# Attention and mixture of experts on one core: each PSUM ring tile a buffer of its own, four tanhs and then one exponential per unit

## The chip, the cores and the metric

The kernel runs on one core of a Trainium2 chip. The metric is the device time in microseconds (us) of one execution; lower is better. Five engines work beside each other, each in the order of its own program, and wait for each other by semaphores: PE (TensorE, matrix multiplies), ACT (ScalarE, tanh, exponential, copies), DVE (VectorE), POOL (GpSimd) and SP (SyncE, which issues most transfers). Matrix products are written to PSUM, a small memory of eight banks.

## The reference, cut to what matters

Soft-capped attention over 4 batches with 12 heads of 448 rows of width 64, and then a mixture of 8 experts in which each of the 1792 rows goes to one expert.

```python
scores = scale * np.matmul(q, k.transpose(0, 1, 3, 2))
scores = cap * np.tanh(scores / cap)
attn = np.exp(scores - np.max(scores, axis=-1, keepdims=True))
attn = attn / (np.sum(attn, axis=-1, keepdims=True) + 1e-09)
out = np.matmul(attn, v)
...
e_idx = np.argmax(x @ w_gate, axis=1)          # x: the attention's rows
for e in range(8):
    h = np.maximum(x[e_idx == e] @ w1[e], 0.0)
    out[e_idx == e] = gate_w * eom * (h @ w2[e])
```

## The kernel before

The attention comes first and takes about half of the time, the experts follow. The attention runs over 24 *units* (4 batches of 6 pairs of heads); the loop over `u` near the end of the kernel writes out by hand the order in which every engine gets its work, and nothing reorders it later.

In iteration `u`, PE computes the scores of unit `u`, transposed, in four tiles: `qk(u, 0)` to `qk(u, 2)` hold two heads times 448 columns for 128 rows of K each (L349), `qk(u, 3)` the last 64 rows of both heads (L354). ACT takes each tile out of PSUM with a tanh (L356) into `pt`, and an exponential (L336, `exps`) runs in place over `pt`: one over the first four chunks of 448 columns after the second tanh, one over the other three after the fourth. Then PE multiplies the exponentials of the unit *before* with V: `pv(u - 1, c)`, 16 records in the trace (L366), called PV below. Its result is copied out by `u_evac` (DVE in units 0 to 7, ACT from 8 on, L385). POOL adds up the exponentials for the row sums (`presum`, L375 to L380), PE sums them over the partitions on every other unit (`sums`, L399). DVE turns and splits K and Q for later units (L294, L284, L290).

In the iterations of the following batch, `slot(u, ...)` puts the work that ends a batch in between: gate products (`tg`, L446), transposes of the sums (`trec`, L430), of the gates (`pg`, L461) and of finished attention rows (`trow`, L540, which DVE scales by `xr`, L544, and SP writes to memory as `xs`), ranks of the rows within their expert (`trk`, L494), and at the end the gathering of rows for the first expert (`gather`, L806; `tx`, L818).

All these products, scores, PV and the slots' work, take their PSUM tiles from one pool, `ps_s`, with three buffers of two banks each (named A, B and C below). `half()` hands out the two banks of a tile to two different uses, one after the other: the fourth score tile and PV, two row transposes, two gate transposes. Waits are by tile: what is written to the second bank waits until the first bank has been read. Which buffer a tile gets is settled when the program is built.

Of the kernel before, what the change touches and what calls it, by code (L numbers as in the profile page):

```python
# [9 lines left out]
F32 = mybir.dt.float32  # L10
# [4 lines left out]
ACTF = mybir.ActivationFunctionType  # L15
# [7 lines left out]
def tile_kernel(ctx: ExitStack, tc, q, k, v, cap, w_gate, w_ogate, w1, w2, out):  # L23
    nc = tc.nc
    B, H, S, D = q.shape
# [55 lines left out]
    ps_s = att.enter_context(tc.tile_pool(name="ps_s", bufs=3, space=PSUM))  # L81
# [3 lines left out]
    def tbank(shape, name):  # L85
        tpools.append(tpools.pop(0))
        return tpools[-1].tile(shape, F32, tag="t", name=name)
# [9 lines left out]
    NK = 3  # L97
# [37 lines left out]
    def load_k(u):  # L135
        if u >= NU:
            return
        t, src = kks[u % 3], heads(k, u)
        for c in range(2):
            pieces(t[:, 0:NB], src[0], c, nc.sync)  # L140
        for c in range(2, 4):
            pieces(t[:, 0:BK], src[1, 0:SK], c, nc.sync)
        for c in range(2, 4):
            pieces(t[:, BK + 2:BK + 4], src[1, SK:S], c, nc.scalar)

    def load_q(u):
        if u >= NU:
            return
        t = ldp.tile([128, 2, NB, 32], F32, tag="lq", name="lq", bufs=2)
        lo = 1 - u % 2  # L150
        for c in range(4):
            h = c // 2 * NP + u % NP
            pieces(t[:, 1 - lo:].rearrange("p h r a -> p (h r) a"), q[u // NP, h:h + lo + 1].rearrange("h s d -> (h s) d"), c, nc.sync)
        for i in range(1 - lo, 2):
            ldq[u + i - (1 - lo)] = t[:, i]

    def load_v(u):
        if u < NU:
            v_ = heads(v, u)
            load_natural(vvs[u % 3], v_, NK, 128, (nc.sync, nc.sync))  # L160
            load_tails(vvs[u % 3], v_, nc.sync)


    capc = const.tile([128, 1], F32, name="capc")
# [48 lines left out]
    for j in range(2):  # L213
        for z, src in ((0, w_gate), (8, w_ogate)):
            nc.gpsimd.dma_start(
                out=wg[64 * j:64 * j + 64, :, j, z:z + 8],
                in_=src.rearrange("(j p d) e -> j d p e", j=2, d=D)[j],
# [10 lines left out]
                        in_=tabi.rearrange("p n c -> p (n c)")[:, 0:DM // 16])  # L228
# [49 lines left out]
    pl, pt, ut, s1, ups, smt, rec, xr, lg = {}, {}, {}, {}, {}, {}, {}, {}, {}  # L278
# [32 lines left out]
    def turn_next(n):  # L311
        for f, u in turns[:n]:
            f(u)
        del turns[:n]

    pair = []

    def half(new=False):
        if new or not pair:
            t = ps_s.tile([128, 2, 512], F32, tag="s", name="s")  # L320
            pair[:] = [t[:, 0], t[:, 1]]
        return pair.pop(0)

    def prep_first():
        pk = tbank([128, SK + 128], "tk0")
# [5 lines left out]
        pl[0] = planes_of(0, pk, "K", SK + 128) + planes_of(0, pq, "Q", S)  # L331
        scales()

    def exps(u, s):
        x = pt[u][:, 4 * s:min(4 * s + 4, 2 * NK + 1)]
        nc.scalar.activation(out=x, in_=x, func=ACTF.Exp, scale=capc)  # L336

    def qk(u, s):
        KH, KL, QH, QL = pl[u]
        if s == 0:  # L340
            pt[u] = ptp.tile([128, 2 * NK + 1, S], F32, tag="pt", name="pt")
        n = 2 if s < NK else 1
        sl = slice(s * 128, (s + 1) * 128)
        if s < NK:
            ps = ps_s.tile([128, 2, 512], F32, tag="s", name="s")
            for i, (x, y) in enumerate(((KH, QH), (KL, QH), (KH, QL))):
                for j in range(2):
                    h = slice(64 * j, 64 * j + 64)
                    nc.tensor.matmul(ps[:, j, 0:S], lhsT=x[h, sl], rhs=y[h], start=(i == 0), stop=(i == 2))  # L349
            ps = ps[:, :, 0:S]  # L350
        else:
            ps = half(True)[:, 0:S]
            for i, (x, y) in enumerate(((KH, QH), (KL, QH), (KH, QL))):
                nc.tensor.matmul(ps, lhsT=x[:, sl], rhs=y, start=(i == 0), stop=(i == 2))  # L354
            ps = ps.unsqueeze(1)
        nc.scalar.activation(out=pt[u][:, 2 * s:2 * s + n], in_=ps, func=ACTF.Tanh, scale=icap)  # L356
        if s % 2:
            exps(u, s // 2)

    def pv(u, c):  # L360
        P = pt[u]
        V = vvs[u % 3]
        if c == 0:
            ups[u] = half()[:, 0:S]
        for j in range(2):
            nc.tensor.matmul(ups[u][64 * j:64 * j + 64], lhsT=V[:, c, j, :], rhs=P[:, 2 * c + (j if c < NK else 0)],  # L366
                             start=(c == 0), stop=(c == NK))

    def presum(u, s):
        P = pt[u]  # L370
        eng = nc.vector if u >= NU - 2 else nc.gpsimd
        if s == 0:
            a = smp.tile([128, 2, S], F32, tag="pa", name="pa")
            s1[u] = smp.tile([128, 2, S], F32, tag="pb", name="pb", bufs=3)
            eng.tensor_tensor(out=a, in0=P[:, 0:2], in1=P[:, 2:4], op=ALU.add)  # L375
            eng.tensor_tensor(out=s1[u], in0=a, in1=P[:, 4:6], op=ALU.add)  # L376
        else:
            for j in range(2):
                h = slice(64 * j, 64 * j + 64)
                eng.tensor_tensor(out=s1[u][h, j], in0=s1[u][h, j], in1=P[h, 2 * NK], op=ALU.add)  # L380

    def u_evac(u):
        t = utp.tile([128, S], F32, tag="ut", name="ut")
        if UACT <= u < NU - 3 or u == NU - 1:
            nc.scalar.activation(out=t, in_=ups.pop(u), func=ACTF.Copy)  # L385
        else:
            nc.vector.tensor_copy(out=t, in_=ups.pop(u))
        ut[u] = t

    def sums(u):  # L390

        b, p = divmod(u, NP)
        if p % 2 == 0:
            return
        r = p // 2
        if r == 0:
            smt[b] = ps_m.tile([128, S], F32, tag="sm", name="sm")
        for g in range(4):
            nc.tensor.matmul(smt[b][32 * g:32 * g + 32], lhsT=ohc[:, r, :], rhs=s1[u - 1 + g // 2][:, g % 2],  # L399
                             start=(r == 0), stop=(r == NP // 2 - 1))  # L400
# [10 lines left out]
    def end_of_batch(b):  # L411
        def bank(shape, name, m=False):
            if b == B - 1:
                return tbank(shape, name)
            if m:
                return ps_m.tile(shape, F32, tag="sm", name=name)
            x = half()[0:shape[0], 0:math.prod(shape[1:])]
            if len(shape) == 2:
                return x
            k = "abc"[:len(shape) - 1]  # L420
            return x.rearrange(f"p ({' '.join(k)}) -> p {' '.join(k)}", **dict(zip(k, shape[1:])))
# [5 lines left out]
        def sums_tr():  # L427
            ps = rt["trec"] = bank([CP, NCH, 4, 32], "trec", b == B - 2)
            for c in range(NCH):
                nc.tensor.transpose(ps[:, c].rearrange("p j n -> p (j n)"),  # L430
                                    rt["ssb"][:, c * CP:(c + 1) * CP], ident)
# [10 lines left out]
        def gate_mm(r):  # L442
            ps = rt["tg"] = bank([128, S], "tg") if b < B - 1 else moe[0].tile([128, S], F32, tag="hph", name="tg")
            for p in range(*grp[r]):
                o0 = 32 * (p - grp[r][0])
                nc.tensor.matmul(ps[o0:o0 + 32], lhsT=wg[:, p].rearrange("p j e -> p (j e)"),  # L446
                                 rhs=ut[b * NP + p], start=True, stop=True)
# [108 lines left out]
        t = [sums_out, L(sums_tr, recips), L(P(gate_mm, 0), P(gate_out, 0)), L(P(gate_mm, 1), P(gate_out, 1))]  # L556
# [345 lines left out]
    def slot(u, y):  # L902
        for f in slots.pop((u, y), ()):
            f()
# [8 lines left out]
    for u in range(NU):  # L913
        for s in range(NK):
            qk(u, s)
        load_k(u + 3)
        if u % 2:
            load_q(u + 3)
        before, after = TURN.get(u, (1, 1))
        turn_next(before)  # L920
        if u > 0:
            presum(u - 1, 1)
        pair.clear()
        slot(u, "f")
        pair.clear()
        slot(u, "g")
        qk(u, NK)
        slot(u, "h")
        if u > 0:
            for c in range(NK + 1):  # L930
                pv(u - 1, c)
        turn_next(after)
        if u > 1 and u - 2 != EARLY:
            sums(u - 2)
        pair.clear()
        slot(u, "q")
        if u > 0:
            u_evac(u - 1)
        load_v(u + 2)
        presum(u, 0)  # L940
        slot(u, "e")
    pair.clear()
    u = NU - 1
    for s in range(NK):
        pv(u, s)
# [244 lines left out]
    split_to(SP0)  # L1190
    bg.extend(end_of_batch(B - 1))
    pv(u, NK)
    u_evac(u)
    tx(0)
# [97 lines left out]
```

## Time and profile before

| | |
|---|---|
| median of 3 runs | 618.85 us (617.74 to 619.21) |
| the profiled execution's own time | 618.58 us |
| its span, first to last instruction | 616.5 us |
| mean granted TensorE clock (1 is 2.4 GHz, 0.5 is 1.2 GHz) | 0.902 |
| PE busy in the span | 534.1 us, 87% |
| ACT, DVE, POOL busy | 376.6, 376.5, 300.6 us |

PE is the engine with the most work. The busy time of a stretch, what an engine waited for in it, and the clock in it tell more than the share over the span, since attention and experts differ.

### The profile page before, as it was taken

What the parts mean: (1) busy time and instruction counts of PE and PEld (TensorE: products, weight loads), DVE (VectorE), ACT (ScalarE), POOL (GpSimd) and SP (SyncE); (2) the same over time, 40 slices, a digit from 0 to 9 for tenths busy, and PEclk for the clock granted to TensorE, in tenths of its full rate; (3) what the DMA queues carried; (4) which work ended last, traced back from release to release, by engine and by line L of the source; (5) the groups of instructions that cost most, each with busy time, mean ns of one, the idle gap of its engine ahead of it and who ended that gap; (6) DMA issues with size and microseconds to landing.
All of it is one profiled execution on the core that took longest, in us unless ns stands there. A gap on an engine that the chain in (4) does not pass through costs nothing. (4 is left out here: it accounts for less than half of the span.)

```text
span 616.5 us, 10153 instructions
## 1 busy us (share of the span) xinstructions
PE 534.1 (87%) x3053; PEld 352.2 (57%) x3053; DVE 376.5 (61%) x627; ACT 376.6 (61%) x449; POOL 300.6 (49%) x347
## 2 busy tenths in 40 slices
PE   7678767767887877788899999999999999999995
PEld 5233322334343343433368999978887886767593
DVE  4544414247654567554789999868766848646460
ACT  6654554427567466544656678868676858646570
POOL 8756353416766555745457256662163732643001
PEclk9778777769788798877899999999999999999998
DMA  7533314154562554433877079253386796997001
GB/s 136 97 63 58 59 36 70 27 105 69 98 74 45 93 104 75 60 64 79 297 261 242 16 274 407 71 180 136 117 354 234 247 409 216 401 301 306 15 27 42
DMA packets 157773, 91.94 MB, mean 149 GB/s; under 512 B 140418, under 2 KB 140554, under 8 KB 157712
## 3 DMA queue, kind: packets, MB, share of 16 engines
q1 hardware_dynamic: 144032, 57.86, 36.6%
q0 software_dynamic: 8832, 32.74, 14.5%
q10 hardware_dynamic: 4848, 0.63, 0.6%
q8 instruction: 26, 0.43, 0.3%
q14 instruction: 35, 0.29, 0.1%
HBM read 123.68 MB, written 12.04 MB: 220 GB/s over the span
## 5 line engine op out<-in xcount | busy, mean ns | idle before, releaser
L994 DVE TENSOR_TENSOR wr<-raw,wr 128x768 fp32r<-128x768 f32 (+1 forms) x167 | 171.9, 1066 | 64.6 <-ACT wr L993 63.5
L993 ACT ACTIVATE wr<-raw 128x768 fp32r<-128x768 f32 (+1 forms) x167 | 150.4, 936 | 33.9 <-PE py L1015 8.6
L366 PE MATMUL s<-pt,vv 128*64 128x448 f32 x384 | 118.6, 783 | 38.4 <-ACT pt L356 38.4
L356 ACT ACTIVATE pt<-s,icap 128x896 f32<-128x896 f32 x96 | 83.4, 905 | 74.9 <-PE s L349 61.7
L366 PEld LDWEIGHTS s<-pt,vv 128*64 128x64 f32 x384 | 35.8, 195 | 109.6 <-issue 58.4
L336 ACT ACTIVATE pt<-pt,capc 128x1792 f32<-128x1792 f32 (+1 forms) x48 | 76.9, 1603 | 1.6
L1015 PE MATMUL py<-wr,hh 128*128 128x384 f32 x352 | 77.3, 341 | 0.0
L1015 PE MATMUL php<-wr,xh 128*128 128x512 f32 x264 | 74.7, 404 | 0.0
L376 POOL TENSOR_TENSOR pb<-pa,pt 128x896 f32<-128x896 f32 x22 | 46.0, 2092 | 57.1 <-PE sm L399 45.7
L1015 PEld LDWEIGHTS py<-wr,hh 128*128 128x128 f32 x352 | 61.2, 188 | 4.0 <-issue 3.7
L375 POOL TENSOR_TENSOR pa<-pt 128x896 f32<-128x896 f32 x22 | 45.9, 2086 | 34.4 <-ACT pt L336 33.7
L1084 POOL DMA_INDIRECT out_dram<-yo,ti x13 | 18.0, 1384 | 89.0 <-ACT yo L1082 63.6
L1015 PEld LDWEIGHTS php<-wr,xh 128*128 128x128 f32 x264 | 47.5, 188 | 12.1 <-issue 2.1
L380 POOL TENSOR_TENSOR pb<-pb,pt 64x448 f32<-64x448 f32 x44 | 49.9, 1135 | 4.2 <-DMA tab<-ent,posi 0.9
L1015 PE MATMUL py<-wr,hl 128*128 128x384 f32 x176 | 44.8, 335 | 0.0
L294 DVE STREAM_TRANSPOSE tk<-kk 128x512 f32<-128x512 f32 x23 | 16.6, 722 | 42.9 <-DMA kk<-in_k_dram 36.0
L1015 PE MATMUL php<-wr,xl 128*128 128x512 f32 x132 | 41.5, 395 | 0.0
L349 PE MATMUL s<-QH,KH 64*128 64x448 f32 x144 | 30.4, 414 | 9.7 <-ACT pt L356 7.3
L385 ACT ACTIVATE ut<-s 128x448 f32<-128x448 f32 x14 | 7.6, 544 | 46.3 <-PE s L366 46.3
L1131 POOL DMA_DIRECT2D rh<-in_moe_w_dram x42 | 23.2, 555 | 21.8 <-DVE wr L994 13.6
L1015 PEld LDWEIGHTS py<-wr,hl 128*128 128x128 f32 x176 | 31.8, 188 | 0.0
L349 PEld LDWEIGHTS s<-QH,KH 64*128 64x128 f32 x144 | 13.7, 184 | 29.5 <-ACT pt L356 10.6
(262 smaller groups left out, 829.7 us busy)
## 6 DMA issues: line engine op xcount, KB each, us to landing
raw<-in_moe_w_dram SPq DMA_DIRECT2D x78, 512.0 KB
raw<-in_moe_w_dram SPq DMA_DIRECT2D x104, 384.0 KB
rh<-in_moe_w_dram POOLq DMA_DIRECT2D x18, 512.0 KB, 7.6
rh<-in_moe_w_dram POOLq DMA_DIRECT2D x24, 384.0 KB, 9.0
lq<-in_q_dram SPq DMA_DIRECT2D x44, 112.0 KB
vv<-in_v_dram SPq DMA_DIRECT2D x48, 96.0 KB
xs<-xr SPq DMA_DIRECT2D x36, 112.0 KB
kk<-in_k_dram SPq DMA_DIRECT2D x46, 56.0 KB
```

Source lines behind the costliest of these rows:

```text
L336: nc.scalar.activation(out=x, in_=x, func=ACTF.Exp, scale=capc)
L349: nc.tensor.matmul(ps[:, j, 0:S], lhsT=x[h, sl], rhs=y[h], start=(i == 0), stop=(i == 2))
L356: nc.scalar.activation(out=pt[u][:, 2 * s:2 * s + n], in_=ps, func=ACTF.Tanh, scale=icap)
L366: nc.tensor.matmul(ups[u][64 * j:64 * j + 64], lhsT=V[:, c, j, :], rhs=P[:, 2 * c + (j if c < NK else 0)], start=(c == 0), stop=(c == NK))
L375: eng.tensor_tensor(out=a, in0=P[:, 0:2], in1=P[:, 2:4], op=ALU.add)
L376: eng.tensor_tensor(out=s1[u], in0=a, in1=P[:, 4:6], op=ALU.add)
L380: eng.tensor_tensor(out=s1[u][h, j], in0=s1[u][h, j], in1=P[h, 2 * NK], op=ALU.add)
L993: nc.scalar.activation(out=t[:, 0, 0:F], in_=raw, func=ACTF.Copy)
L994: nc.vector.tensor_tensor(out=t[:, 1, 0:F], in0=raw, in1=t[:, 0, 0:F].bitcast(F32), op=ALU.subtract)
L1015: nc.tensor.matmul(ps[g][:, 0:n], lhsT=st[:, c], rhs=w[:, z, g * n:(g + 1) * n], start=(c == 0 and st is hi and z == 0), stop=(c == (KD, K ...
L1084: nc.gpsimd.indirect_dma_start(out=out, out_offset=bass.IndirectOffsetOnAxis(ap=ti, axis=0), in_=y, in_offset=None, bounds_check=NT - 1, o ...
L1131: nc.gpsimd.dma_start(out=d, in_=rows_of(src, e, w, c), **kw)
```

## The change

`half` now takes a whole tile of the ring for each use, and `pair`, which held the second bank back, is gone: PV, each row transpose and each gate transpose have a tile of their own. `exps` is gone: the four tanhs of a unit come one after the other, and one exponential runs over all seven chunks (3136 columns) after the fourth.

```diff
-    pair = []
-
-    def half(new=False):
-        if new or not pair:
-            t = ps_s.tile([128, 2, 512], F32, tag="s", name="s")
-            pair[:] = [t[:, 0], t[:, 1]]
-        return pair.pop(0)
+    def scores(name):
+        return ps_s.tile([128, 2, 512], F32, tag="s", name=name)
+
+    def half(name):
+        return scores(name)[:, 0]
...
-    def exps(u, s):
-        x = pt[u][:, 4 * s:min(4 * s + 4, 2 * NK + 1)]
-        nc.scalar.activation(out=x, in_=x, func=ACTF.Exp, scale=capc)
...
-            ps = half(True)[:, 0:S]
+            ps = half("s3")[:, 0:S]
...
         nc.scalar.activation(out=pt[u][:, 2 * s:2 * s + n], in_=ps, func=ACTF.Tanh, scale=icap)
-        if s % 2:
-            exps(u, s // 2)
+        if s == NK:
+            nc.scalar.activation(out=pt[u], in_=pt[u], func=ACTF.Exp, scale=capc)
...
         if c == 0:
-            ups[u] = half()[:, 0:S]
+            ups[u] = half("u")[:, 0:S]
...
-            x = half()[0:shape[0], 0:math.prod(shape[1:])]
+            x = half(name)[0:shape[0], 0:math.prod(shape[1:])]
```

The calls of `pair.clear()` in the loop are gone too. Lines from here on stand five or more lower in the changed kernel.

On ACT, in iteration 5, before the change (`kk` is a small transfer of K that ACT issues between its third and fourth tanh):

```order
L356 ACTIVATE pt<-s,icap 128x896 x2
L336 ACTIVATE pt<-pt,capc 128x1792
L356 ACTIVATE pt<-s,icap 128x896
L132 DMA kk_123<-in_k_dram 32x2x32 x2
L356 ACTIVATE pt<-s,icap 128x448
L336 ACTIVATE pt<-pt,capc 128x1344
```

and in the same iteration after it (tanh is L351, the exponential L353, `s_819` the fourth tile):

```order
L351 ACTIVATE pt<-s,icap 128x896 x3
L132 DMA kk_122<-in_k_dram 32x2x32 x2
L351 ACTIVATE pt<-s_819,icap 128x448
L353 ACTIVATE pt<-pt,capc 128x3136
```

The exponential of the first chunks no longer stands between the second and the third tanh; the transfer keeps its place.

On PE, in iteration 5, the fourth score tile and PV before, with the semaphores that each waits for:

```order
L354 MATMUL s_747<-QH_660,KH_607 128x448 [waits Activation_49]
L354 MATMUL s_747<-QH_660,KL_608 128x448
L354 MATMUL s_747<-QL_661,KH_607 128x448
L366 MATMUL s_747<-pt_626,vv1_126 64x448 [waits DMAHW3_49,Activation_49]
L366 MATMUL s_747<-pt_626,vv1_126 64x448 [waits DMAHW4_49]
```

and after:

```order
L349 MATMUL s3_745<-QH_658,KH_606 128x448 [waits Activation_49]
L349 MATMUL s3_745<-QH_658,KL_607 128x448
L349 MATMUL s3_745<-QL_659,KH_606 128x448
L361 MATMUL u_751<-pt_625,vv1_126 64x448 [waits DMAHW3_49,Activation_49]
L361 MATMUL u_751<-pt_625,vv1_126 64x448 [waits DMAHW4_49]
```

PV had the tile of the fourth scores and waited for their tanh (the Activation semaphore); now it has a tile of its own, `u_751`, and waits for the tanh of whatever was in that buffer before, here the third scores.

On PE, in iteration 12, the three large score tiles before:

```order
L349 MATMUL s_1312<-QH_1195,KH_1153 128x448 [waits PE_49]
L349 MATMUL s_1312<-QH_1195,KH_1153 128x448
L349 MATMUL s_1312<-QH_1195,KL_1154 128x448 x2
L349 MATMUL s_1312<-QL_1196,KH_1153 128x448 x2
L349 MATMUL s_1320<-QH_1195,KH_1153 128x448 [waits DVE_49]
L349 MATMUL s_1320<-QH_1195,KH_1153 128x448
L349 MATMUL s_1320<-QH_1195,KL_1154 128x448 x2
L349 MATMUL s_1320<-QL_1196,KH_1153 128x448 x2
L349 MATMUL s_1329<-QH_1195,KH_1153 128x448 [waits Activation_49]
```

and after:

```order
L344 MATMUL s_1314<-QH_1196,KH_1152 128x448 [waits DVE_49,Activation_49]
L344 MATMUL s_1314<-QH_1196,KH_1152 128x448
L344 MATMUL s_1314<-QH_1196,KL_1153 128x448 x2
L344 MATMUL s_1314<-QL_1197,KH_1152 128x448 [waits DVE_49]
L344 MATMUL s_1314<-QL_1197,KH_1152 128x448
L344 MATMUL s_1322<-QH_1196,KH_1152 128x448 [waits Activation_49]
L344 MATMUL s_1322<-QH_1196,KH_1152 128x448
L344 MATMUL s_1322<-QH_1196,KL_1153 128x448 x2
L344 MATMUL s_1322<-QL_1197,KH_1152 128x448 x2
L344 MATMUL s_1330<-QH_1196,KH_1152 128x448 [waits Activation_49]
```

Before, the three tiles lay in three buffers, and the last waited for the copy of PV's result; after, all three lie in one buffer, and the second and the third each wait for the tanh of the tile before.

The buffers (A, B, C) of all tiles as the two programs have them, by iteration: the three large score tiles, the slots' tiles before the fourth, the fourth score tile and PV, and the slots' tiles behind PV (g gates, r sums, w rows, p gate transposes, k ranks):

```
 u  before                      after
 0  C B A | -     | C -  | -    C B A | -     | C -  | -
 1  B A C | -     | B B  | -    B A C | -     | B A  | -
 2  A C B | -     | A A  | -    C B A | -     | C B  | -
 3  C B C | -     | A A  | -    A C A | -     | C A  | -
 4  B C B | -     | C C  | -    C B C | -     | B C  | -
 5  B A B | -     | A A  | -    B A B | -     | A B  | -
 6  B C B | -     | C C  | Bg   A C A | -     | C A  | Cg
 7  A A A | -     | A A  | Bg   B B B | -     | B B  | Cg
 8  C C C | Cr    | B B  | -    A A A | Cr    | A B  | -
 9  A C A | Cw    | A A  | -    A C A | Cw Aw | B B  | -
10  B C A | Bp    | C C  | -    B C A | Bp Cp | A A  | -
11  B A C | Bw    | A A  | -    B C A | Bw Cw | A A  | -
12  C B A | Ck    | B B  | Ag   A A A | Ak Bw | C C  | Ag
13  C B A | Cw    | B B  | Ag   C B C | Bw    | C C  | Ag
14  C B A | Cr    | B B  | -    C C C | Cr    | B B  | -
15  C A B | Cw    | A A  | -    A B A | Bw Cw | A A  | -
16  B C A | Bp    | C C  | -    A A A | Ap Bp | C C  | -
17  B A C | Bw    | A A  | -    C A B | Cw Aw | B B  | -
18  C B A | Ck    | B B  | Ag   B B B | Bk Cw | A A  | Bg
19  C B A | Cg Bw | A A  | Cp   A C A | Cg Aw | B B  | Bp Cp
20  B A C | Bw    | A A  | -    A A B | Cw Aw | B C  | -
21  C B A | Ck    | B B  | -    A B C | Ak Bw | C C  | -
22  A C B | Aw    | C C  | Bw   A B C | Aw Bw | C C  | Aw
23  A B C | -     | A A  | -    B A C | -     | B A  | -
```

A lone tile before (Cw, Bp, Ck) holds two of the slots' pieces in its two banks.

## Rows read from the trace of the kernel before

**Rows 1.** Windows, attention and experts: us, busy time by engine, TensorE clock, DMA share, GB/s

```profile
0.00:307.00 307.00, 232.49 (x1182) 108.34 (x1183) 157.53 (x319) 171.77 (x174) 172.05 (x178) 0.81 0.45 84
330.00:400.00 70.00, 70.00 (x381) 63.52 (x380) 63.81 (x122) 54.09 (x73) 38.78 (x46) 1.00 0.55 200
```

The busy times are those of PE, PE's weight loads, DVE, ACT and POOL, each with its count of instructions.

**Rows 2.** Waits of PE, 0 to 306 us: total, times, longest

```profile
PE s L366 <- ACT pt L356: 38.4, 23, 3.4
PE s L540 <- DVE xr L544: 12.9, 6, 6.8
PE s L349 <- ACT pt L356: 7.3, 9, 1.2
PE s L354 <- ACT pt L356: 4.2, 6, 1.4
PE s L540 <- DVE rk L509: 3.3, 3, 1.2
...
PE s L461 <- DVE gm L468: 2.4, 3, 0.9
```

**Rows 3.** Timeline of PE, iteration 5: start, duration, ..., idle before and releaser

```profile
60.32 0.47 PE L349 MATMUL s<-QH,KH 64*128 64x448 f32 x2
...
62.34 0.47 PE L349 MATMUL s<-QH,KH 64*128 64x448 f32 x2 [0.54 <-ACT pt L356]
...
66.49 6.12 PE L366 MATMUL s<-pt,vv 128*64 128x448 f32 x16 [2.36 <-ACT pt L356]
```

**Rows 4.** Timeline of ACT, iteration 5 (two tanhs in the first row)

```profile
61.28 1.91 ACT L356 ACTIVATE pt<-s,icap 128x896 f32<-128x896 f32 x2 [4.21 <-PE s L349]
...
63.22 1.79 ACT L336 ACTIVATE pt<-pt,capc 128x1792 f32<-128x1792 f32 x1
...
66.47 1.42 ACT L336 ACTIVATE pt<-pt,capc 128x1344 f32<-128x1344 f32 x1
```

**Rows 5.** Timeline of PE, iteration 7, three score tiles in one buffer

```profile
87.15 0.47 PE L349 MATMUL s<-QH,KH 64*128 64x448 f32 x2 [1.16 <-ACT pt L356]
...
89.13 0.53 PE L349 MATMUL s<-QH,KH 64*128 64x448 f32 x2 [1.10 <-ACT pt L356]
...
94.06 5.98 PE L366 MATMUL s<-pt,vv 128*64 128x448 f32 x16 [0.72 <-ACT pt L356]
```

**Rows 6.** PV: one of iteration 10 (timeline); all, windows of L366 (PE, weight loads, clock)

```profile
142.37 3.23 PE L366 MATMUL s<-pt,vv 128*64 128x448 f32 x16 [0.72 <-ACT pt L356]
...
0.00:84.60 84.60, 31.88 (x96) 9.37 (x96) 0.80 0.47 82
...
0.00:307.00 307.00, 118.59 (x384) 35.81 (x384) 0.81 0.45 84
```

**Rows 7.** Groups of ACT by form: busy, mean ns of one, idle before

```profile
L336 ACT ACTIVATE pt<-pt,capc 128x1792 f32<-128x1792 f32 x24 | 43.0, 1790 | 0.8
L336 ACT ACTIVATE pt<-pt,capc 128x1344 f32<-128x1344 f32 x24 | 34.0, 1416 | 0.8
```

**Rows 8.** Timeline of DVE and PE, iteration 9

```profile
124.70 0.73 DVE L294 STREAM_TRANSPOSE tk<-kk 128x512 f32<-128x512 f32 x1 [6.74 <-DMA vv<-in_v_dram]
...
127.53 1.10 PE L540 MATMUL s<-ident,ut 128*112 128x128 f32 x4 [6.82 <-DVE xr L544]
```

**Rows 9.** End of the attention: SP, POOL, PE (timelines); landing of xg

```profile
279.95 6.54 SPq L791 DMA_DIRECT2D tc<-tab  x8
...
287.72 5.61 SPq L549 DMA_DIRECT2D xs<-xr  x6
...
296.07 1.26 POOL L806 DMA_INDIRECT xg<-xs,ti  x1 [8.91 <-DMA xs<-xr]
...
DMA to landing us min/median/max: 5.4/7.8/9.2
...
306.61 0.87 PE L818 MATMUL pt_x<-ident,xg 128*128 128x128 f32 x6
```

**Rows 10.** Waits of DVE, 0 to 306 us

```profile
DVE tk L294 <- DMA kk<-in_k_dram: 36.0, 9, 9.7
```

More of the change, by code (lines that the diff above doesn't have):

```diff
@@ L344, in qk @@
         if s < NK:
-            ps = ps_s.tile([128, 2, 512], F32, tag="s", name="s")
+            ps = scores("s")
             for i, (x, y) in enumerate(((KH, QH), (KL, QH), (KH, QL))):
@@ L922, in tile_kernel @@
             presum(u - 1, 1)
-        pair.clear()
         slot(u, "f")
-        pair.clear()
         slot(u, "g")
@@ L934, in tile_kernel @@
             sums(u - 2)
-        pair.clear()
         slot(u, "q")
@@ L941, in tile_kernel @@
         slot(u, "e")
-    pair.clear()
     u = NU - 1
```

## The prediction

> **What bounds the kernel now.** I read the windows first. From 330 us on PE is busy in every microsecond at full clock, and the change touches nothing there [rows 1]. In the attention, 0 to 307 us, PE is busy 232.5 us, no other engine over 172.1, and PE's mean granted clock is 0.81 [rows 1]: no engine is full, PE waits, and part of the time it computes at 1.2 instead of 2.4 GHz. The experts follow on the same engine, so a microsecond taken from the attention's end is one taken from the total, as long as the experts' first data are there.
>
> The list of PE's waits shows on whom: 38.4 us in PV on a tanh, 12.9 in row transposes on `xr`, 7.3 and 4.2 in score tiles on a tanh, 3.3 on `rk`, 2.4 on `gm` [rows 2]. These six, together 68.5 us, all come from the ring. The timelines of iteration 5 show the largest: PE starts the scores at 60.32 and PV only at 66.49, after an idle 2.36 [rows 3]; ACT meanwhile does two tanhs from 61.28, an exponential of 1.79, two tanhs, and at 66.47 the second exponential [rows 4]. PV needs nothing of this unit but the bank, which the fourth tanh frees. Thus the first exponential lies on the path to PV.
>
> The other part is the clock. PV takes 3.23 us in iteration 10 and 6.12 in iteration 5, and all 24 take 118.59 [rows 3, 6]. At 3.23 each they would take 77.5, so 41 us are half clock. Iteration 7 shows that the wait directly ahead does not decide alone: there 0.72 stands ahead of PV as in iteration 10, but PV takes 5.98, after score tiles that had waited 1.16 and 1.10 [rows 5, 6].
>
> **The change part by part.** The sum is made against the profiled execution's 618.58 us (span 616.5), which is 0.04% under the median of 618.85, so it needs no correction. Within 0.3%, 1.9 us, I call no change, about what a measurement here can tell.
>
> *The exponential.* The third tanh now follows the second at once: in iteration 5 that is 1.79 us earlier. One exponential over 3136 columns is not in the trace; the two forms differ by 448 columns and 0.374 us (1790 and 1416 ns [rows 7]), and so 1.416 + 4 × 0.374 = 2.91, against 3.21 for the pair. Bounds: 2.91 if the line goes on, 3.21 if nothing is saved. Either way it lies beside PV (3.23 and more) and ACT has 172 of 307 us of work; I cost it at nothing. What it delays: POOL's sums start later by up to 1.8 us, and POOL is as little loaded as ACT. Without that cover the cost would be 1.8 per unit. On ACT the small K transfer keeps its place ahead of the fourth tanh and comes earlier with it; the copy of PV's result stands behind the exponential, but has to wait for PV anyway.
>
> *PE's waits.* Buffers decide them, and the table of buffers falls into three groups. **Group 1**, iterations 1 to 6 and 23: the fourth tile and PV lie in different buffers, PV in that of an earlier score tile whose tanh is done or nearly. I take from iterations 3 to 6 the 0.54 at the third tile [rows 3], some 0.2 at the fourth and 0.4 at PV, 1.15 each, and 0.3 in iterations 1, 2 and 23: 5.6 us in all (floor 0; at the old 0.72 ahead of every PV, 9). **Group 2**, iterations 9 to 11, 13, 15, 17, 19, 21, 22: the fourth tile and PV still share one buffer, so that PV waits for the fourth tanh as before, 0.72 at least [rows 6], but the tanh is not late any more; with some 0.9 at tiles before it 1.6, times 9 = 14.4. **Group 3**, iterations 7, 8, 12, 14, 16, 18: three score tiles go through one buffer, and each waits for the tanh of the one before: 1.16 + 1.10 [rows 5], about 1.35 at the next tile in that buffer (the longest such wait is 1.4 [rows 2]) and 0.72, 4.3 × 6 = 25.8. In iterations 12, 14, 16 and 18 this is new. Iteration 20 is mixed: 2.0. Sum 47.8, against 68.5: **−20.7**. In it the waits on `xr`, `rk` and `gm` are gone, since the second row transpose has a buffer of its own and the next writer of the first comes later. The longest was 6.82, in iteration 9, where `xr` stood on DVE behind a K transpose that waited for its load [rows 8]. What is late next there is the score or PV tile that gets this buffer; by the table it comes behind other tiles, and I count it in the 0.9.
>
> *PV's own time.* Iterations 1 to 6: 31.88 in six [rows 6]. With the hole ahead of PV closed I expect the 3.23 of iteration 10 from the third on and 5.5 and 3.5 for the first two: 21.9, **−10**. Bounds: 31.9 (nothing) and 19.4. The others take 118.59 − 31.88 = 86.7 now. I take 5.9 for group 3 (iteration 7 [rows 5]), 4.1 for group 2 (between iteration 10 and that, nearer iteration 10, since it waits as little), 11.8 for iterations 20, 23 and the last PV: 35.4 + 36.9 + 11.8 = 84.1, **−2.6**.
>
> *The scores of group 3.* With waits between them they run partly at the lower clock; a pair of matmuls takes 0.47 to 0.53 there and when cold twice its pace. I charge 0.9 us an iteration, 5 in all: **+5** (0 if they stay warm; 2 an iteration, 12, if all are cold).
>
> *The end.* The first expert needs gathered rows. From SP's table reads at 279.95 (6.54 us of issuing) follow SP's writes of `xs` at 287.72 (5.61), POOL's gather at 296.07, its landing 5.4 to 7.8 later, and PE's use at 306.61 [rows 9]. The rows have landed by 301.5 to 303.9, so that only 2.7 to 5.1 us of slack lie between. The beginning of this chain moves up with all that was gained before, but iterations 21 to 23 would by the terms above give about 10 us more behind it, of which the chain lets about 5 through: **+5**, and PE then waits at L818 for `xg`. Bounds: 0 to +7.
>
> Sum: −20.7 − 10 − 2.6 + 5 + 5 = −23.3; 618.58 − 23.3 = **595 us**.
>
> **The rivals.** *The clock stays up throughout.* If the ring's short holes do not lower the clock, all 24 PVs take 3.23 (77.5, 28.5 less than the 106.0 above) and the 5 us of cold scores are gone: 595 − 33 = 562, some 565 after the end chain. For it: iteration 10. Against: iteration 7 has just these holes and PV at half clock [rows 5]. Chance 0.08.
>
> *The transfers hold the attention.* DVE waits 36.0 us for loads of K [rows 10]. If the first iterations are paced by their loads, −23 becomes nothing, 618, or half of it, 606. Against it: in rows 3 PE waits for ACT and not for planes, and the loads are issued from queues that move up with the iterations. Chance 0.12, most of it near 606.
>
> *The slower side: the clock stays down.* In group 3 PE works in bursts of about 0.9 us between holes of 1.1 [rows 5]. If from iteration 7 on the granted clock does not come back up between such iterations, the 18 PVs take 6.1 each, 110 in place of 84.1 (+26), and their scores some 20 more: 595 + 46 = 641. It decides from about half of that on (+23). For it: iterations 12, 14, 16 and 18 had three buffers and now have one, and iteration 7's PV at 5.98. Against it: before, group 2's PVs recovered within one or two iterations of iteration 7, and iteration 10 ran at 3.23 [rows 6]. Chance 0.06.
>
> The Trainium skill has this as a mechanism ("TensorE: Matmul & The Clock Gate", section "A second HAM failure mode: psum-queue depth-cycling"): a kernel that cycles its PSUM banks makes PE idle briefly between groups of matmuls, often enough that the clock swings between half and full rate. Iteration 7 agrees with it, with 5.98 us for a PV that takes 3.23 elsewhere; by this rule alone the time would be the 641 of this rival.
>
> *The change doesn't do what it says.* In group 2 PV still shares its buffer with the fourth scores; if the tanh's lead is used up elsewhere there, nine times 1.8 us come back: 611. Chance 0.06, with the shares of the next part.
>
> **How the numbers follow.** The forecast, 595 with its own bounds (PV of iterations 1 to 6 from 19.4 to 31.9, cold scores 0 to 12, end 0 to 7, not all at one end: 584 to 606), has 0.68. The rest is the clock up 0.08 (565), transfers 0.12 (606 to 618), clock down 0.06 (641), group 2 unhelped 0.06 (611). The range of 8 in 10 reaches from 581 to 609: it takes in the forecast and half of the transfers' case. Faster takes all but the clock down (0.06), a fourth of the transfers' case (0.03) and 0.02 for the end of mine: 0.89. No change 0.04, slower 0.07.
>
> **What would show it right or wrong.** After the change PE's wait of PV for a tanh falls from 38.4 to 10 or 12 us; L540 no longer waits for `xr`; one exponential of about 2.9 us stands 24 times; PV takes about 106 in all and 22 in iterations 1 to 6; iterations 12, 14, 16, 18 show the second and third score tile waiting 1.1 each; PE waits some 5 us for `xg` at the transposes of the first expert; the attention ends near 283. Wrong would be: PV over 115 in all (clock down), K or Q planes (`KH`, `QH`) among PE's waits by over 10 us (transfers), or PV at half clock in iterations 1 to 6 although it waits less than 1 us.

## The result and the profile after

| | before | after |
|---|---|---|
| median | 618.3 us (617.48 to 619.21, 4 runs) | 586.97 us (583.21 to 590.41, 4 runs) |
| ratio, with its 95% interval | | 0.949 (0.943 to 0.956) |
| span of the profiled execution | 616.5 us | 583.9 us |
| mean granted TensorE clock | 0.902 | 0.936 |
| end of the last PV | 306.68 us | 272.45 us |

The change is 5.1% faster. 595 was forecast, with 581 to 609 as the range. The attention ends 34.2 us earlier and the span is 32.6 us shorter, so the gain lies where it was looked for, and the experts keep it but for 1.6 us.

The windows of the kernel after, as in [rows 1] (PE, weight loads, DVE, ACT, POOL; clock, DMA share, GB/s), first the attention, then a stretch of it, then the experts:

```profile
0.00:272.45 272.45, 219.30 (x1178) 106.33 (x1178) 153.78 (x317) 167.97 (x149) 170.67 (x175) 0.87 0.49 91
...
17.00:60.00 43.00, 39.03 (x233) 17.47 (x231) 28.80 (x45) 35.70 (x29) 38.22 (x25) 1.00 0.62 107
...
300.00:370.00 70.00, 69.92 (x380) 63.20 (x379) 63.81 (x113) 54.45 (x73) 39.31 (x46) 1.00 0.53 191
```

PE's idle time in the attention is 272.45 − 219.30 = 53.2 us. Before it was 307.00 − 232.49 = 74.5 [rows 1], so 21.3 are gone, and the other 13 are busy time: the same matmuls at a higher clock. Iterations 2 to 6 (17 to 60 us) run at full clock without a break.

PE's waits after the change (total, times, longest), to be read beside [rows 2]; L344 are the three large score tiles, L349 the fourth, L361 PV, L535 the row transposes:

```profile
PE s L344 <- ACT pt L351: 20.6, 21, 1.8
PE u L361 <- ACT pt L351: 11.0, 18, 0.7
PE trow L535 <- ACT pt L351: 3.8, 5, 2.2
...
PE u L361 <- DVE xr L539: 2.8, 1, 2.8
PE s L349 <- ACT pt L351: 2.3, 5, 1.1
...
PE pt_x L813 <- DMA xg<-xs,ti: 1.3, 1, 1.3
```

PV's wait has fallen from 38.4 to 11.0 and none of these is over 0.7. The row transposes wait no more for `xr`; PV does once, 2.8 us. In return the large score tiles wait 20.6 us for a tanh, in place of 7.3.

Iteration 5 on ACT and on PE (timeline: start, duration, ..., idle before and what ended it), as in [rows 3, 4]:

```profile
43.88 3.00 ACT L351 ACTIVATE pt<-s,icap 128x896 f32<-128x896 f32 x3 [0.71 <-PE s L344]
...
46.79 0.63 ACT L351 ACTIVATE pt<-s,icap 128x448 f32<-128x448 f32 x1
47.45 2.92 ACT L353 ACTIVATE pt<-pt,capc 128x3136 f32<-128x3136 f32 x1
...
42.91 0.47 PE L344 MATMUL s<-QH,KH 64*128 64x448 f32 x2
...
44.95 0.48 PE L344 MATMUL s<-QH,KH 64*128 64x448 f32 x2 [0.55 <-ACT pt L351]
...
46.94 3.23 PE L361 MATMUL u<-pt,vv 128*64 128x448 f32 x16 [0.23 <-ACT pt L351]
```

PV starts 4.03 us after the first score matmul instead of 6.17, behind a hole of 0.23 instead of 2.36, and takes 3.23 us instead of 6.12. The exponential now lies beside PV.

Iteration 12 is one of those in which the ring sends three score tiles through one buffer:

```profile
113.41 0.47 PE L344 MATMUL s<-QH,KH 64*128 64x448 f32 x2
...
115.44 0.47 PE L344 MATMUL s<-QH,KH 64*128 64x448 f32 x2 [1.16 <-ACT pt L351]
...
117.42 0.47 PE L344 MATMUL s<-QH,KH 64*128 64x448 f32 x2 [1.10 <-ACT pt L351]
...
119.39 0.18 PE L489 MATMUL trk<-ohb,tri 112*112 112x32 bf16 x1 [1.10 <-ACT pt L351]
...
122.16 5.37 PE L361 MATMUL u<-pt,vv 128*64 128x448 f32 x16 [0.72 <-ACT pt L351]
```

It is iteration 7 of before over again [rows 5]: four holes, and behind them PV at 5.37. PV alone, windows of L361 (PE, weight loads, clock, DMA share, GB/s), iterations 1 to 6 and all, beside [rows 6], and ACT's group of the new exponential, beside [rows 7]:

```profile
0.00:58.40 58.40, 19.36 (x96) 6.36 (x96) 0.97 0.64 112
0.00:275.00 275.00, 93.92 (x384) 29.97 (x384) 0.87 0.49 92
...
L353 ACT ACTIVATE pt<-pt,capc 128x3136 f32<-128x3136 f32 x24 | 69.8, 2910 | 0.8
```

### The profile page after: what moved, and what is told of

It reads as the page before. It is cut to its first block, busy times and chain, and to the rows that moved or that the text cites. A ratio compares the mean times of both kernels' runs of the same rounds, so it can differ in the third digit from the quotient of the medians.

```text
span 583.9 us, 10115 instructions
## 1 busy us (share of the span) xinstructions
PE 521.4 (89%) x3053; PEld 350.5 (60%) x3053; DVE 373.4 (64%) x627; ACT 372.9 (64%) x425; POOL 299.2 (51%) x347
## 5 line engine op out<-in xcount | busy, mean ns | idle before, releaser
L351 ACT ACTIVATE pt<-s,icap 128x896 f32<-128x896 f32 x96 | 84.3, 912 | 74.1 <-PE s L344 43.1
L361 PE MATMUL u<-pt,vv 128*64 128x448 f32 x384 | 93.9, 641 | 13.9 <-ACT pt L351 11.0
L1006 PE MATMUL php<-wr,xh 128*128 128x512 f32 x264 | 74.7, 404 | 0.0
L361 PEld LDWEIGHTS u<-pt,vv 128*64 128x64 f32 x384 | 30.0, 162 | 70.8 <-issue 43.4
L353 ACT ACTIVATE pt<-pt,capc 128x3136 f32<-128x3136 f32 x24 | 69.8, 2910 | 0.8
L1075 POOL DMA_INDIRECT out_dram<-yo,ti x13 | 20.1, 1548 | 92.4 <-ACT yo L1073 68.2
L344 PE MATMUL s<-QH,KH 64*128 64x448 f32 x144 | 32.4, 445 | 24.3 <-ACT pt L351 20.6
L344 PEld LDWEIGHTS s<-QH,KH 64*128 64x128 f32 x144 | 13.9, 188 | 48.9 <-ACT pt L351 31.1
L526 POOL DMA_INDIRECT tab<-ent,posi x16 | 16.0, 1002 | 30.9 <-issue 14.6
```

The source lines that it names most:

```text
L353: nc.scalar.activation(out=pt[u], in_=pt[u], func=ACTF.Exp, scale=capc)
L1006: nc.tensor.matmul(ps[g][:, 0:n], lhsT=st[:, c], rhs=w[:, z, g * n:(g + 1) * n], start=(c == 0 and st is hi and z == 0), stop=(c == (KD, K ...
L1075: nc.gpsimd.indirect_dma_start(out=out, out_offset=bass.IndirectOffsetOnAxis(ap=ti, axis=0), in_=y, in_offset=None, bounds_check=NT - 1, o ...
```

## The experiments

My theory was that the place of the exponential makes the gain, that the ring's buffers decide what is left of it, and that holes in PE's work (stretches in which it waits) carry a second price, the lower clock behind them. The rival for the first is that the gain comes from the tiles of their own; for the last, that PV is slow there for another reason. All ratios are against the kernel before, with 95% intervals, from five rounds each.

| kernel | exponential | tiles | ring | median, us | ratio |
|---|---|---|---|---|---|
| before | split, early | shared | as built | 616 to 618 | 1 |
| own_tiles | split, early | own | as built | 629.26 | 1.020 (1.017 to 1.023) |
| one_exp | one, late | shared | as built | 590.48 | 0.956 (0.953 to 0.960) |
| changed_again | one, late | own | as built | 585.74 | 0.954 (0.951 to 0.958) |
| split_late | split, late | own | as built | 584.64 | 0.949 (0.945 to 0.952) |
| rotate_pairs | one, late | shared | in turn | 568.58 | 0.919 (0.915 to 0.923) |
| rotate_early_exp | split, early | own | in turn | 573.60 | 0.926 (0.922 to 0.930) |
| rotate | one, late | own | in turn | 549.93 | 0.892 (0.889 to 0.896) |
| rotate_rows_first | one, late | own | in turn | 540.59 | 0.874 (0.872 to 0.877) |

**The halves of the change.** own_tiles is the changed kernel with this in place of the one exponential:

```diff
-        if s == NK:
-            nc.scalar.activation(out=pt[u], in_=pt[u], func=ACTF.Exp, scale=capc)
+        if s % 2:
+            x = pt[u][:, 2 * s - 2:min(2 * s + 2, 2 * NK + 1)]
+            nc.scalar.activation(out=x, in_=x, func=ACTF.Exp, scale=capc)
```

> Own tiles alone: PV and the slots' pieces have a tile each as in the changed kernel, but the exponential is still split, four chunks after the second tanh and three after the fourth. My theory: the first exponential (1.79 us) stays on the way to the third and fourth tanh. The second row transposes no longer wait for xr (12.9 us before), but PV still waits about 1.4 us in iterations 1 to 6 (for the third tanh, which comes late) and 1 to 2.4 us where it shares the buffer with the fourth tile; PV stays at half clock in many iterations, 105 to 115 us in all. Time 600 to 612. Rival, that the buffers are what brought the gain and the exponential hardly matters: 585 to 592.

It came out slower than the kernel before, outside the ranges of both theories. PV's wait for a tanh did shrink (38.4 to 16.6 us), but the early exponential still stands ahead of the third tanh, and with own tiles more of PE's other work waits for a tanh: the large score tiles 19.0 us in place of 7.3, the fourth tiles 15.6 in place of 4.2. The timelines of own_tiles in iterations 11 and 12 (the exponential is ACT's L354, PV is L362, the fourth tile PE's L349):

```profile
129.99 1.79 ACT L354 ACTIVATE pt<-pt,capc 128x1792 f32<-128x1792 f32 x1
...
131.69 0.99 ACT L351 ACTIVATE pt<-s,icap 128x896 f32<-128x896 f32 x1
...
132.73 0.64 PE L349 MATMUL s<-QH,KH 128*128 128x448 f32 x1 [2.07 <-ACT pt L351]
134.84 5.62 PE L362 MATMUL u<-pt,vv 128*64 128x448 f32 x16 [0.72 <-ACT pt L351]
...
148.00 1.10 PE L536 MATMUL trow<-ident,ut 128*112 128x128 f32 x4 [1.67 <-ACT pt L351]
```

The delay of 2.07 now stands ahead of the fourth tile, and PV, in the same buffer as that, waits 0.72 more. Over the attention, which ends at 318.96 us, PE is idle for 74.7 us, as long as before (74.5): the waits have only moved. The loss is in PE's busy time, 244.28 us in place of 232.17. PV takes 4.1 us less (114.45), but all score matmuls together 12.1 more (78.34 to 90.47), at a mean clock of 0.79. My estimate had counted waits at PV alone and no slower scores.

one_exp is the kernel before with the one exponential; the halves stay:

```diff
-        if s % 2:
-            exps(u, s // 2)
+        if s == NK:
+            nc.scalar.activation(out=pt[u], in_=pt[u], func=ACTF.Exp, scale=capc)
```

> The exponential alone: four tanhs, then one exponential, with the tiles of the kernel before, in which the fourth scores and PV share a tile and two row transposes share one. My theory: PV waits 0.72 us in each of 23 iterations (17 us in place of 38.4), the waits on xr stay near 12.9, and since the buffers still go round in iterations 12 to 18 nearly all PVs run at full clock, 80 to 88 us in all. Time 583 to 593, about as the whole change. Rival, that PV needs its own tile to start early and without one the clock stays low as before (0.72 ahead of each PV as in iteration 7): PV 105 us or more, time 605 or more.

The time is as expected and not far from that of the whole change: the exponential makes most of the gain. The attention ends at 278.44 us, which is 28.2 of the 34.2 us. The two sizes in the expectation were off, though. PV takes 97.4 us and the row transposes wait 25.1 us for `xr`, I think because they are reached sooner (waits of PE in one_exp):

```profile
PE s L540 <- DVE xr L544: 25.1, 6, 7.8
PE s L366 <- ACT pt L356: 18.2, 23, 1.5
```

split_late cuts the one exponential in two, both behind the fourth tanh:

```diff
-            nc.scalar.activation(out=pt[u], in_=pt[u], func=ACTF.Exp, scale=capc)
+            for x in (pt[u][:, 0:4], pt[u][:, 4:7]):
+                nc.scalar.activation(out=x, in_=x, func=ACTF.Exp, scale=capc)
```

> The changed kernel with its one exponential cut in two again, four chunks and three, but both behind the fourth tanh. My theory: it is the place of the exponential that counts; the 0.30 us more on ACT per unit lie beside PV, time as the changed kernel within its spread, 584 to 591. Rival, that the saved 0.3 us of the single instruction count on the path (24 x 0.3 = 7 us): 591 to 597.

No loss: the place of the exponential counts, not the instruction that is saved.

**The ring taken in turn.** rotate gives every tile of the ring, the first `tq0` included, the next of three fixed buffers:

```diff
+    nth = [0]
+
     def scores(name):
-        return ps_s.tile([128, 2, 512], F32, tag="s", name=name)
+        nth[0] += 1
+        return ps_s.tile([128, 2, 512], F32, tag=f"s{nth[0] % 3}", name=name, bufs=1)
```

> The changed kernel with the ring taken strictly in turn, A, B, C, A, ..., so that no iteration puts three score tiles through one buffer. My theory: in iterations 7, 8, 12, 14, 16, 18 the waits of about 1.1 us between score tiles and the 1.4 at the next tile go (20.6 us at score tiles falls under 8), and with them the half clock after them: PV 78 to 83 us in all in place of 93.9, scores 5 us less. Together 25 to 40 us: 547 to 562. Rival 1, the loads or the planes on DVE become the bound: the waits on tanh go, but waits on KH, QH or xr take their place, 570 or more. Rival 2, the half clock does not come from these holes: PV stays over 90 us, and only the waits of 13 us or so are gained, 573.

It is the first theory, near the lower end of its range: 36 to 37 us less than the two medians of the changed kernel. Not a single large score tile waits for a tanh any more (waits of PE in rotate; L347 the large tiles, L364 PV):

```profile
PE u L364 <- DVE xr L542: 17.2, 4, 5.2
PE trow L538 <- ACT pt L354: 7.1, 10, 3.6
PE s L347 <- DVE ut L385: 5.9, 5, 2.5
...
PE s L352 <- ACT pt L354: 2.7, 11, 0.3
```

Iteration 12 there, to set beside that of the changed kernel above:

```profile
110.09 0.47 PE L347 MATMUL s<-QH,KH 64*128 64x448 f32 x2
...
113.03 0.65 PE L538 MATMUL trow<-ident,ut 128*112 128x128 f32 x4 [0.65 <-ACT pt L354]
113.93 0.47 PE L352 MATMUL s<-QH,KH 128*128 128x448 f32 x1 [0.25 <-ACT pt L354]
...
114.73 3.23 PE L364 MATMUL u<-pt,vv 128*64 128x448 f32 x16
```

From the first score matmul to PV it is 4.64 us instead of 8.75. All PVs take 87.4 us, not the 78 to 83 expected. Four of them now wait for `xr` in their buffer, 17.2 us together, and take 4.6 to 5.4 us each. Two more, in iterations 3 and 5, take 4.92 and 4.77 behind a score tile that waited 1.69 and 2.52 us for `ut`.

rotate_rows_first takes most of the wait for `xr` away by DVE's order, from iteration 8 on:

```diff
-        before, after = TURN.get(u, (1, 1))
+        before, after = TURN.get(u, (1, 1) if u < NP + 2 else (0, 2))
```

> The kernel with the strict rotation (rotate), and from iteration 8 on both of DVE's turns of K and Q stand behind PV in program order, so that xr no longer stands behind a K transpose. Theory: the 17.2 us that PV waits for xr in rotate come from DVE's order; they fall under 5 and the half clock behind them goes too: 535 to 544. Rival: xr only waits for the same late loads one place further on, or PE now waits for the planes (KH, QH): 548 or more.

Measured 540.59, the fastest of all. PV's wait on `xr` is 6.8 us, somewhat over the 5 expected; two more waits ahead of PV, 4.6 us together, have no releaser in the profile. The clock over the attention, which ends at 225.80 us, is 0.96.

rotate_pairs and rotate_early_exp put one half of the change back under the rotation. The second is rotate with the diff of own_tiles, the first is one_exp with this, where `scores` is that of rotate and serves the large score tiles and `tq0` too:

```diff
     def half(new=False):
         if new or not pair:
-            t = ps_s.tile([128, 2, 512], F32, tag="s", name="s")
+            t = scores()
```

> The strict rotation and the one late exponential, but the tiles shared as before the change (fourth scores and PV, two row transposes, two gate transposes in the halves of one). Theory: own tiles are worth something once the ring goes round: here PV waits 0.72 in each iteration (17 us) and the second row transposes wait for xr (25 us in one_exp), so 562 to 578. Rival, that own tiles bring nothing even then, since they only use up the ring sooner: 552 or less.

> The strict rotation with the exponential split as before the change (four chunks after the second tanh). Own tiles alone were slower than the kernel before (629); my explanation is that the ring's single buffers made PE wait for the third tanh, which the early exponential delays by 1.79 us. Under the rotation the fourth tile waits for the first tanh and PV for the second, where no slot tile stands between, so the delay counts only in some nine iterations with two slot tiles and a part of the others: 562 to 575. Rival, that the early exponential lies on the path in every unit (24 x 1.79 = 43 us): 590 or more; and if it doesn't matter at all, 550.

Both came out inside the first range. So with the late exponential own tiles are worth about 3% (0.919 to 0.892) once the ring goes round. In the ring as built they are worth about 1% at most: the whole change has 0.954 here and 0.949 in the first measurement, one_exp 0.956, and split_late, which ran beside one_exp, 0.949. The early exponential costs 3.4 points under the rotation, where, but for one, only iterations with the slots' tiles feel it: the fourth tile (L352) waits 24.8 us for a tanh, 15 times, in place of 2.7.

**The clock.** Rotation takes away holes and their waits together. Two runs keep the waits and only give PE something to do in them; in iterations 7, 12, 16 and 18 small matmuls write 64 columns that nobody reads:

```diff
+        if u in (7, 12, 16, 18) and s < NK - 1:
+            for i in range(8):
+                nc.tensor.matmul(smt[(u - 2) // NP if u != 7 else 0][:, S:512], lhsT=KH[:, sl], rhs=QH[:, 0:512 - S],
+                                 start=False, stop=False)
```

> The changed kernel with 8 small idle matmuls (64 columns into unused columns of the row sums' bank, read by nobody) in each of the two holes between the score tiles of iterations 7, 12, 16 and 18. They shorten no wait; they only keep PE at work in it. If the holes lower the clock: PV of these iterations falls from 21.1 us together (5.5, 5.4, 5.3, 4.9) to 13 to 15 and their scores by 2 to 4, time 576 to 582. Rival, that the lower clock has another reason, such as what else runs there, or comes with the waits themselves: PV as before and 586 to 591.

Median 580.40, ratio 0.938 (0.934 to 0.942). The time moved as the theory said. The four PVs did not: in the one execution with a trace they take 19.6 us together, not the 13 to 15 expected. That execution took 586.11 us and the others 576 to 583, so it does not speak for them, and this run decides nothing on the clock. filled_more does it behind all four score tiles, in the place of `if u in ... s < NK - 1` and `range(8)`:

```diff
+        if u in (7, 12, 16, 18):
+            for i in range(8 if s < NK else 5):
```

> As filled_holes, and with small idle matmuls also behind the third score tile (8) and behind the fourth (5) of iterations 7, 12, 16 and 18, so that the hole of about 1.1 us ahead of the fourth tile and most of the 0.72 ahead of PV are filled too. No wait gets shorter. If the holes set the clock: the four PVs, 21.1 us together in the changed kernel and 19.6 with the first two holes filled, fall to 13 to 16, and the time to 572 to 580. Rival, that the wait itself or the other engines' work lowers the clock: PVs stay at 5 us, time as the changed kernel or a little over it for the added matmuls.

> The changed kernel once more, beside the next run, since its first four times spread from 583 to 590: 583 to 591, median near 587.

The windows of the four PVs (PE, weight loads, clock, DMA share, GB/s; the last line sums up), in changed_again:

```profile
67.60:73.40 5.80, 5.62 (x16) 1.72 (x16) 0.57 0.47 86
123.30:128.60 5.30, 5.10 (x16) 1.54 (x16) 0.63 0.76 152
175.90:182.20 6.30, 6.11 (x16) 1.71 (x16) 0.53 0.07 16
201.70:207.00 5.30, 5.15 (x16) 1.59 (x16) 0.62 1.15 192
sum 22.70, PE 21.97 PEld 6.56; mean PE 5.49 PEld 1.64
```

and in filled_more:

```profile
68.60:73.00 4.40, 4.17 (x16) 1.33 (x16) 0.77 0.51 97
124.10:128.00 3.90, 3.73 (x16) 1.24 (x16) 0.86 0.99 190
173.60:177.00 3.40, 3.23 (x16) 1.06 (x16) 1.00 0.81 166
195.00:198.30 3.30, 3.23 (x16) 1.06 (x16) 1.00 1.07 158
sum 15.00, PE 14.35 PEld 4.69; mean PE 3.59 PEld 1.17
```

The same PVs, behind the same tanhs, take 14.35 us instead of 21.97. Iteration 14 also sends three tiles through one buffer, and there the holes were left as they are; in the same execution its PV stays slow (timeline of PE in filled_more):

```profile
147.51 5.70 PE L364 MATMUL u<-pt,vv 128*64 128x448 f32 x16 [0.72 <-ACT pt L351]
```

So the holes lower the clock, shown by filling them. The time did not follow all the way: 582.64, ratio 0.948 (0.945 to 0.951), against 0.954 (0.951 to 0.958) for changed_again beside it, which misses the 572 to 580 expected. The four PVs gain 7.6 us, but the attention ends only 4.9 sooner (262.93 against 267.81) and the span is only 3.5 shorter. A part is given back behind the PV of iteration 18, where PE waits 3.3 us for `rk`, which it does not in changed_again. The wait for the first expert's rows is nearly the same in both (6.6 and 6.2 us). Why filled_holes, which fills less, has the better ratio stays open.

## Why the prediction was right, point by point

**The exponential.** 2.91 us was forecast for it and 2910 ns measured. It lies beside PV in the timeline, and split_late shows that some 0.3 us more of it in each unit cost nothing. That it was on PV's path before is shown by one_exp.

**PE's waits.** −20.7 was forecast and −21.3 is the idle time that went. The groups came out as described: PV waits 0.23 in iteration 5 (group 1), 0.72 ahead of most others, and group 3, but for iteration 8, has its holes of 1.16, 1.10, 1.10 (1.35 in iteration 18) and 0.72. That the total fits so well is in part luck. The holes in the timeline, without those on `wz`, `QH` and issue, add up to 3.2 us in group 1 (5.6 forecast, from terms that make 5.5), 15.6 in group 2 (14.4), 22.9 in group 3 (25.8) and 5.9 in iteration 20 (2.0): 47.6 against 47.8, and the misses cancel. That the waits of group 3 are a fault of the ring and no need of the work was not in the prediction; rotate shows it.

**PV's own time: the term that was mis-sized.** −10 and −2.6 were forecast, −12.5 and −12.1 measured (31.88 to 19.36 in iterations 1 to 6, 86.7 to 74.6 in the rest). I had charged 5.5 and 3.5 to the first two PVs, which both take 3.23. Of the rest the largest miss is group 3, 28.9 us in place of 35.4: five of its PVs take 4.6 to 5.5 instead of 5.9, and that of iteration 8 takes 3.26. There I had read the table too coarsely: the transposes of the sums fill the time ahead of the fourth tile, and PV has another buffer, so that only the two holes of 1.16 and 1.10 are left. Group 2 takes 34.2 in place of 36.9. I had charged 4.1 to each of its PVs, of which six of nine run at 3.23 in this profile and all nine in that of changed_again. A hole of 0.72 alone does not slow those: in iteration 7 of before [rows 5] there were three holes before that. I had read that row rightly and then still priced group 2 between the two. The three slow ones of this profile are iterations 15 and 22, behind a hole of 1.82 and one of 2.22, and 21, whose holes are all short; what slowed that one stays open.

**The scores of group 3.** +5 was forecast. All score matmuls went from 54.36 + 23.98 to 59.30 + 26.96 us, +7.9, and the slots' products got some 2.5 us slower, which was not in the sum. I put both down to the lower clock behind the holes: the transposes of the gates take 2.76 us in iteration 16, behind three holes, and 1.86 in iteration 10.

**The end.** +5 was forecast, +1.6 measured in the first profile, of which 1.34 is PE's wait for `xg`. The attention was to end near 283; without the +5, which lies behind it, the sum's own terms make 278.4 (306.68 − 28.3), and it ended at 272.45. The chain is there all the same. In changed_again the last PV ends at 267.81, 4.6 us sooner than in the first profile, and the span is still 584.5 (timeline of PE in changed_again):

```profile
264.58 3.23 PE L361 MATMUL u<-pt,vv 128*64 128x448 f32 x16 [0.25 <-ACT pt L353]
274.03 1.54 PE L813 MATMUL pt_x<-ident,xg 128*128 128x128 f32 x6 [6.22 <-DMA xg<-xs,ti]
```

What PE gains in the last iterations is given back as a wait of 6.22 us.

In sum: −21.3 (waits), −24.7 (PV), +7.9 (scores), +2.5 (slots), some +1.4 for the rest, and +1.6 behind the attention make −32.6 us, against −23.3. PV gained 12.1 us more than forecast; the scores, the slots and the rest took 6.8 of it back, so that the misses partly cancel, and the end cost 3.4 less.

**The rivals.** The transfers did not hold: PE waits 3.0 us for planes of Q, against 2.4 before. Group 2 was helped: no PV in it waits longer than 0.72. The clock did not stay down: behind iteration 7 it comes back, and iterations 9 to 11 have PV at 3.23. (Before the change it had taken a little longer than the prediction says: PV took 5.91 and 4.85 in iterations 8 and 9, and 3.23 in 10.) The Trainium skill's rule ("TensorE: Matmul & The Clock Gate", "A second HAM failure mode: psum-queue depth-cycling") has PE's short idles between groups of matmuls make the clock swing between half and full rate. The four PVs of changed_again, at clocks of 0.53 to 0.63, agree with it. The 641 of the prediction took the clock to stay down for the whole stretch, and it did not: between the iterations of group 3 PV mostly runs at 3.23. The clock staying up throughout did not come either, but the miss lies on its side: PV took 93.9 us, between the 106 forecast and the 77.5 of this rival.

## What to carry to other kernels

Before pricing a change of buffers, write down which buffer each tile gets and who read it last: the edit that gives each use a tile of its own was a loss by itself (+2.0%, with the early exponential), worth about 1% at most with the late one, and a gain of 3% with the late one once the ring went round. The table of buffers shows which iterations pay for it. A long instruction in the middle of a train that frees buffers belongs behind the train, if other work covers it there. Count a hole in PE's work twice: as a wait, and as the slower matmuls that may follow, above all when several holes come close together.

## What was not expected of the hardware

In iteration 10 after the change one hole of 0.72 us ahead of PV left it at 3.23 us, in a stretch (82 to 115 us) with a clock of 1.00. In changed_again three of about 1.1 us or more and one of 0.72 in one iteration brought PV to 5.1 to 6.1 us, at mean clocks of 0.53 to 0.63 between the two levels, 1.2 GHz (0.5) and 2.4 GHz (1). Matmuls that do nothing useful, in the same holes, brought it back to 3.23 to 4.17.

The size of the holes in an iteration does not settle it alone. In one_exp iterations 4 and 5 have the same two, 0.54 or 0.55 at the third score tile and 0.78 or 0.77 ahead of PV, and PV runs at full clock in one and not in the other (timeline of PE in one_exp):

```profile
42.30 3.23 PE L366 MATMUL s<-pt,vv 128*64 128x448 f32 x16 [0.78 <-ACT pt L356]
...
50.04 4.92 PE L366 MATMUL s<-pt,vv 128*64 128x448 f32 x16 [0.77 <-ACT pt L356]
```

What makes the difference there no run shows.
